# One table load, a sigmoid first, and other owners for the magnitudes of the weights

## The chip, the cores and the metric

The kernel runs on one core of a Trainium2 chip. The core has a matrix engine (TensorE, PE in the profile), VectorE (DVE), ScalarE (ACT), GpSimd (POOL) and SyncE (SP), which work side by side and wait for each other through semaphores. Times are device microseconds (us) of one execution; a kernel's time is the median of its runs. Lower is better.

## The reference

Sigmoid attention over 8 batches and 12 heads, sequence 448, head dimension 64, and an MLP on its output:

```python
scores = scale * np.matmul(q, k.transpose(0, 1, 3, 2)) - np.log(S)
attn = 1.0 / (1.0 + np.exp(-scores))
attn_out = np.matmul(attn, v)                       # -> x: (3584, 768)
h = x @ w_in                                        # 768 x 2048
g = np.where(h >= 1, h, np.where(h <= -1, 0.0, (h + 1) ** 2 / 4))
out = g @ w_out                                     # 2048 x 768
```

Inputs and output are float32.

## The kernel before

**The work.** A pair of heads fills the 128 partitions, so a batch is 6 pairs, 48 in all; each pair has four pieces of scores (three of 128 keys and one of 64). The MLP's inner dimension is cut into 16 chunks of 128. "Ups" multiply x by a chunk of w_in, "bend" applies the clipped quadratic, "downs" multiply by w_out. From the third batch on, the ups are done in blocks (L666). For the matmuls of ups and downs the operands are scaled and split into an fp16 high and low part.

**The weights.** The float32 weights arrive as words of 64 bits, two chunks' slots per transfer, in slots that borrow w_out's place in the on-chip memory (`w_out_sb`) or a `raww` tile. Chunk by chunk, `Weight.convert` does this for w_in (`wi`) and later for w_out (`wo`), with f the chunk:

- ScalarE's Prelu turns the high word into a float (L222);
- one step later VectorE shifts and merges the low word (L228, L229), and for some chunks takes the largest magnitude (L233, a reduce);
- one step after that, for the other chunks (`summed`), ScalarE takes the sum of magnitudes with an Abs and an accumulator (L215).

`find_scale` takes the scale of a group of eight chunks from these magnitudes, and `split` writes the fp16 parts: ScalarE the high one (L264), VectorE the low one (L265); for some chunks GpSimd takes part (L260 to L262). The transfers of w_in and the first four of w_out are issued by SP (L199), the later ones of w_out on ScalarE's own queue, from within `convert`. SP's slots must be free again: a slot of w_in's words is free when L229 has read it.

**The start.** Batch 0's attention uses float32 matmuls (L385 scores, L476 times v). ScalarE's sigmoid (L432) stands between the two, and its output of a pair is copied out (L482). In the same time w_in is converted. When batch 0's x is complete, `finish_x` splits it into `xhl`: ScalarE's L499, VectorE's L500. Then PE runs the ups (L700) and downs (L736) of batch 0, and w_out is converted beside them. From pair 8 on q, k and v are scaled and split as well; their magnitudes are ScalarE's L322 (into `hl` or `dump`), their split is L351.

**The second batch.** After batch 0's first downs come the ups of batch 1. Each chunk takes 18 matmuls L700 into one of three `ph` buffers; bend empties it: ScalarE L713, VectorE L714 and L715, then L716 and L717. In the same time VectorE computes the mixed weights for the later batches (L610 to L633), splits w_out (L265) and takes the maxima of x (L486).

**What sets the order.** A scheduler with a model of the machine sets the order of each engine's instructions, except where the code pins it: SP in the first part is in the order of the code, and what is passed to `tc.keep_in_program_order` keeps its place relative to the code's order.

Of the kernel before, what the change touches and what calls it, by code (L numbers as in the profile page):

```python
# [14 lines left out]
F32 = mybir.dt.float32  # L15
F16 = mybir.dt.float16
BF16 = mybir.dt.bfloat16
I32 = mybir.dt.int32
AF = mybir.ActivationFunctionType
# [4 lines left out]
P = 128  # L24
# [7 lines left out]
NFULL = 8  # L32
NHALF = 6

NA = 8
# [10 lines left out]
POOL_FROM = 6  # L46
WI_SUM = 2
WO_SUM = 0
MAX_ACT = 47
# [23 lines left out]
def sigmoid_attention_mlp(ctx: ExitStack, tc: tile.TileContext, first_qvk, qkv, w_in, w_out, out_t):  # L73
# [24 lines left out]

    nls = const.tile([P, 1], F32, name="nls")
    nc.vector.memset(nls, -math.log(S))  # L100


# [73 lines left out]
    class Weight:  # L176


        def __init__(self, dram, sb, name, spare):
            self.dram, self.sb, self.name, self.spare = dram.bitcast(I32), sb, name, spare  # L180
            self.words, self.at, self.loaded = {}, 0, 0
            self.scale, self.inv = [], []
            self.most = const.tile([P, 2, NFC], F32, name=name + "_most")
            nc.vector.memset(self.most, 0.0)
            mod = WI_SUM if name == "wi" else WO_SUM
            self.summed = [f for f in range(NFC) if mod and f % mod == 0 and f not in (NA - 1, NFC - 1)]

# [19 lines left out]
        def convert(self):  # L207

            f = self.at - 2
            if 0 <= f < NFC:  # L210
                w = self.words.pop(f)
                if f in self.summed:

                    dump = wo.f32(-1) if self is wi else w[:, :DM].bitcast(F32)
                    nc.scalar.activation(dump, self.f32(f), AF.Abs, accum_out=self.most[:, 1, f : f + 1])  # L215
                if self is wo:
                    self.load(3 if f == 3 else 1)
            f = self.at
            if f < NFC:

                high = self.words_of(f)[1].bitcast(F32)
                nc.scalar.activation(self.f32(f), high, AF.Prelu, scale=2.0**-112, alpha=-(2.0**32))  # L222
            f = self.at - 1
# [84 lines left out]
    def prep_a(p):  # L308
        if NFULL <= p < NPAIR and first_time("max", p):
# [3 lines left out]
            if p < MAX_ACT:  # L313
# [6 lines left out]
                for t in range(n):  # L320
                    rt = raws[p][:, t * S : 2 * S + VW if t == 2 else (t + 1) * S]
                    nc.scalar.activation(dump[:, : rt.shape[1]], rt, AF.Abs, accum_out=m[:, t : t + 1])  # L322
            for mt, rt in parts[: n - 1] if p >= MAX_ACT else ():
# [482 lines left out]
    with tc.manual_schedule(engines={mybir.EngineType.SP}):  # L806
# [6 lines left out]
        for i in range(LAG):  # L813
            scores([i])
        state["scored"] = LAG
        while at < NPIECE:
# [128 lines left out]
```

## Time and profile before

| | |
|---|---|
| median of 3 runs | 1183.58 us (1179.28 to 1185.38) |
| profiled execution | 1182.99 us, its span 1181.3 us |
| PE busy | 1146.3 us (97%) |
| VectorE busy | 824.9 us (70%) |
| ScalarE busy | 697.1 us (59%) |
| GpSimd busy | 321.6 us (27%) |
| mean granted clock of TensorE | 0.987 |

A line of the profile names the engine, the line of the kernel, the operation, the tile that is written and the tiles that are read; in brackets stands the idle time of the engine just before, and what ended it. "PEld" is the load of weights, which overlaps PE. "PEclk" is the granted clock as a share of full speed. A stretch's row gives each engine's busy time in it.

### The profile page before, as it was taken

Reading aid. Unit: us, or ns where it says so; the run is one execution under the profiler, and the core shown is the slowest. Engines: PE = TensorE matmul, PEld = TensorE weight load, DVE = VectorE, ACT = ScalarE, POOL = GpSimd, SP = SyncE. Lnnn points to the kernel's source line nnn. Section 1 sums busy time; section 2 is a strip of 40 time slices with the busy share of each in tenths; the row PEclk is TensorE's granted clock in tenths of the full one; section 3 lists DMA queues with packets and bytes.
Section 4 is the critical chain, followed back from the end, with each engine's and each line's share of the span. In section 5 each row is a group of like instructions: output and inputs, shape, how many; then the busy total and the mean of one; then the engine's idle time right before and its main releaser. Section 6 shows DMA issues by size and latency. Waiting matters only on the chain.

```text
span 1181.3 us, 20203 instructions
## 1 busy us (share of the span) xinstructions
PE 1146.3 (97%) x7662; PEld 669.0 (57%) x7662; DVE 824.9 (70%) x1760; ACT 697.1 (59%) x1158; POOL 321.6 (27%) x389
## 2 busy tenths in 40 slices
PE   5889999899999999999999999999999999999998
PEld 1224433344445776457755677457764677558954
DVE  4877999898945588467973689466883678736830
ACT  5975885665743587447763577546874486513410
POOL 0004310000332254325354236232534253310000
PEclk8899999899999999999999999999999999999999
DMA  9941544447532366224643165424552146302400
GB/s 361 335 150 61 195 149 132 151 142 244 176 109 64 119 213 212 64 64 150 253 146 100 33 251 193 132 64 141 196 207 68 61 155 223 117 25 98 153 16 32
DMA packets 58113, 170.01 MB, mean 144 GB/s; under 512 B 8608, under 2 KB 39840, under 8 KB 51872
## 3 DMA queue, kind: packets, MB, share of 16 engines
q1 hardware_dynamic: 56288, 159.29, 39.4%
q10 hardware_dynamic: 1728, 9.44, 2.3%
q8 instruction: 60, 0.98, 0.3%
q14 instruction: 37, 0.30, 0.1%
HBM read 126.94 MB, written 23.40 MB: 127 GB/s over the span
## 4 chain that ended last, share of the span: by engine, by line
PE 76%; DVE 9%; DMA 8%; ACT 4%; issue 1%; POOL 1%; SPq 0%; ACTq 0%; DVEq 0%
PE po L736 35%; PE ph L666 23%; PE pav L476 8%; PE psc L394 3%; PE psc L403 3%; DMA blocks<-mixs 2%; PE ph L700 2%; DMA w_out_sb<-w_in 2%; PE psc L389 1%; DMA raw<-qkv 1%; ACT a L432 1%; DVE g L714 1%; DMA w_out_sb<-w_out 1%; DMA w_in_sb<-blocks 1%; DVE mixs L624 1%
## 5 line engine op out<-in xcount | busy, mean ns | idle before, releaser
L736 PE MATMUL po<-ghl,w_out_sb 128*128 128x448 f16 x2304 | 445.7, 353 | 0.9 <-DVE g L715 0.9
L736 PEld LDWEIGHTS <-w_out_sb 128*128 128x128 f16 x2304 | 221.8, 98 | 216.6 <-issue 14.0
L666 PE MATMUL ph<-w_in_sb 128*128 128x224 f16 x3024 | 307.7, 259 | 2.0 <-DMA w_in_sb<-blocks 1.6
L666 PEld LDWEIGHTS <-w_in_sb 128*128 128x128 f16 x3024 | 282.6, 98 | 30.9 <-issue 27.4
L444 DVE SCALAR_TENSOR_TENSOR ahl<-psc,ahl 128x896 f16<-128x896 f32 (+1 forms) x170 | 152.9, 900 | 112.7 <-ACT ahl L443 110.4
L435 ACT ACTIVATE psc<-psc,nls,sqk 128x896 f32<-128x896 f32 (+1 forms) x136 | 129.4, 971 | 114.7 <-PE psc L403 97.2
L356 POOL TENSOR_SCALAR raw<-raw,qkv_s 128x448 f32<-128x448 f32 (+1 forms) x93 | 71.3, 781 | 452.9 <-DVE qkv_i L136 363.0
L443 ACT ACTIVATE ahl<-psc 128x896 f16<-128x896 f32 (+1 forms) x170 | 126.9, 762 | 32.9 <-DVE ahl L444 31.8
L700 PE MATMUL ph<-xhl,w_in_sb 128*128 128x448 f16 x576 | 115.5, 358 | 5.2 <-DVE xhl L500 2.9
L675 DVE TENSOR_TENSOR xhl<-ph,xhl 128x224 f32<-128x224 f32 x240 | 87.7, 382 | 26.2 <-PE ph L666 19.7
L322 ACT ACTIVATE dump<-raw 128x448 f16<-128x448 f32 (+1 forms) x105 | 61.8, 588 | 69.0 <-DMA raw<-qkv 68.0
L476 PE MATMUL pav<-ahl,v 128*64 128x448 f16 x748 | 95.6, 359 | 0.0
L713 ACT ACTIVATE g<-xhl,hr,ihr 128x448 f32<-128x448 f32 x96 | 68.7, 752 | 44.0 <-DVE xhl L675 43.1
L716 ACT ACTIVATE ghl<-g 128x448 f16<-128x448 f32 x128 | 72.7, 573 | 36.7 <-DVE g L715 36.3
L700 PEld LDWEIGHTS <-w_in_sb 128*128 128x128 f16 x576 | 55.9, 99 | 64.0 <-issue 16.4
L717 DVE TENSOR_TENSOR ghl<-g,ghl 128x448 f16<-128x448 f32 x128 | 85.6, 675 | 7.1 <-ACT ghl L716 6.6
L714 DVE SCALAR_TENSOR_TENSOR g<-g,rk 128x448 f32<-128x448 f32 x112 | 81.1, 739 | 10.7 <-ACT g L713 10.5
L746 DVE TENSOR_SCALAR o<-po,od 128x448 f32<-128x448 f32 x48 | 32.5, 679 | 65.8 <-PE po L736 65.6
L358 POOL TENSOR_TENSOR hl<-raw,hl 128x448 f16<-128x448 f32 x62 | 70.0, 1149 | 0.0
L394 PE MATMUL psc<-qk 128*128 128x448 f16 x252 | 66.6, 354 | 0.4 <-issue 0.3
L715 DVE SCALAR_TENSOR_TENSOR g<-xhl,ihs,g 128x448 f32<-128x448 f32 x96 | 65.5, 699 | 0.3
L385 PE MATMUL psc<-ghl 64*128 64x448 f32 (+1 forms) x128 | 37.4, 672 | 21.9 <-ACT a L432 17.1
(156 smaller groups left out, 1150.0 us busy)
## 6 DMA issues: line engine op xcount, KB each, us to landing
w_in_sb<-blocks SPq DMA_DIRECT2D x48, 1344.0 KB, 6.5
raw<-qkv SPq DMA_DIRECT2D x34, 704.0 KB, 4.9
qk<-hl SPq DMA_DIRECT2D x320, 56.0 KB, 2.0
w_out_sb<-w_in SPq DMA_DIRECT2D x16, 768.0 KB, 10.9
out_t<-o SPq DMA_DIRECT2D x48, 224.0 KB, 1.9
blocks<-mixs SPq DMA_DIRECT2D x8, 768.0 KB, 4.3
w_out_sb<-w_out ACTq DMA_DIRECT2D x6, 768.0 KB, 4.3
raww<-w_out ACTq DMA_DIRECT2D x6, 768.0 KB, 5.4
```

What stands on the lines that cost most here:

```text
L394: nc.tensor.matmul(out, kq[:, j, 1, w], kq[:, j, 0, :], start=True, stop=False)
L435: nc.scalar.activation(a, a, AF.Sigmoid, bias=nls, scale=sqk)
L443: nc.scalar.activation(hi, x, AF.Copy, scale=ATT)
L444: nc.vector.scalar_tensor_tensor(out=lo, in0=x, scalar=ATT, in1=hi, op0=ALU.mult, op1=ALU.subtract)
L476: nc.tensor.matmul(pav[j * D : (j + 1) * D, :S], *terms[j][t], start=c == 0 and t == 0, stop=mid and t == len(terms[j]) - 1,)
L666: nc.tensor.matmul(out, w[:, wt, wh, c * P : (c + 1) * P], xc[:, xt, c, xh, :], start=j in (0, 2) and c + wh + xh == 0, stop=c == HC - 1 a ...
L675: add = lambda out, q, other: nc.vector.tensor_tensor(out=out, in0=quarter(q), in1=other, op=ALU.add)
L700: nc.tensor.matmul(ph[:, :S], w_in_sb[:, f, wh, c * P : (c + 1) * P], xhl[:, c, xh, :], start=c == 0 and wh + xh == 0, stop=c == NCC - 1 a ...
L714: nc.vector.scalar_tensor_tensor(out=g, in0=g, scalar=rt, in1=g, op0=ALU.min, op1=ALU.mult)
L716: nc.scalar.activation(hi, g, AF.Copy)
L717: (nc.gpsimd if f % GPOOL else nc.vector).tensor_tensor(out=ghl[:, f, 1, :], in0=g, in1=hi, op=ALU.subtract)
L736: nc.tensor.matmul(po[:, :S], w_out_sb[:, f, wh, m * P : (m + 1) * P], ghl[:, f, gh, :], start=f == lo and wh + gh == 0, stop=f == hi - 1 ...
```

## The change

The constant tile `nls` gets a second column, and a sigmoid of one column stands ahead of all else on ScalarE. `scores([0])` is followed at once by the first conversion step, whose Prelu is pinned, so that the first real sigmoid stands ahead of it. The chunks whose magnitudes ScalarE takes are now listed: 8, 10, 12 of w_in (before 0, 2, 4, 6, 8, 10, 12, 14) and ten of w_out (before none). They are taken four steps after the Prelu and not two, are pinned in the order of the code, and write to a `tmp` tile for w_out. The raw maxima of the pairs 8 to 10 are pinned too.

```diff
-WI_SUM = 2
-WO_SUM = 0
+SUMS = (8, 10, 12), (0, 1, 2, 3, 4, 8, 9, 10, 11, 12)
+SUM_LAG = 4
...
-    nls = const.tile([P, 1], F32, name="nls")
+    nls = const.tile([P, 2], F32, name="nls")
     nc.vector.memset(nls, -math.log(S))
+    nc.scalar.activation(nls[:, 1:2], nls[:, 0:1], AF.Sigmoid)
+    nls = nls[:, 0:1]
...
-            mod = WI_SUM if name == "wi" else WO_SUM
-            self.summed = [f for f in range(NFC) if mod and f % mod == 0 and f not in (NA - 1, NFC - 1)]
+            self.summed = SUMS[name == "wo"]
...
         def convert(self):
+            f = self.at - SUM_LAG
+            if f in self.summed:
+                dump = wo.f32(-1) if self is wi else tmp_p.tile([P, S], F32, tag="tmp", name="dump").bitcast(F16)[:, :DM]
+                tc.keep_in_program_order(
+                    nc.scalar.activation(dump, self.f32(f), AF.Abs, accum_out=self.most[:, 1, f : f + 1])
+                )
             f = self.at - 2
             if 0 <= f < NFC:
-                w = self.words.pop(f)
-                if f in self.summed:
-                    dump = wo.f32(-1) if self is wi else w[:, :DM].bitcast(F32)
-                    nc.scalar.activation(dump, self.f32(f), AF.Abs, accum_out=self.most[:, 1, f : f + 1])
+                self.words.pop(f)
                 if self is wo:
                     self.load(3 if f == 3 else 1)
             f = self.at
             if f < NFC:
                 high = self.words_of(f)[1].bitcast(F32)
-                nc.scalar.activation(self.f32(f), high, AF.Prelu, scale=2.0**-112, alpha=-(2.0**32))
+                ins = nc.scalar.activation(self.f32(f), high, AF.Prelu, scale=2.0**-112, alpha=-(2.0**32))
+                if self is wi and f == 0:
+                    tc.keep_in_program_order(ins)
...
-                    nc.scalar.activation(dump[:, : rt.shape[1]], rt, AF.Abs, accum_out=m[:, t : t + 1])
+                    ins = nc.scalar.activation(dump[:, : rt.shape[1]], rt, AF.Abs, accum_out=m[:, t : t + 1])
+                    if p < NFULL + 3:
+                        tc.keep_in_program_order(ins)
...
         for i in range(LAG):
             scores([i])
+            if i == 0:
+                convert(wi, 1)
```

The lines of the changed kernel are shifted: L222 is L226 there, L322 is L328, L351 is L359, L432 is L440, L499 and L500 are L507 and L508, L610 is L618, L714 and L715 are L722 and L723.

The head of ScalarE's list, before (L222 the Prelu, L432 the sigmoid, L215 the Abs, `a` the sigmoid's output):

```order
L222 ACT_TABLE_LOAD
L222 ACTIVATE w_in_sb<-w_out_sb 128x768
L432 ACT_TABLE_LOAD
L432 ACTIVATE a_123<-psc,nls 128x896
L215 ACTIVATE w_out_sb,wi_most<-w_in_sb 128x768
L432 ACTIVATE a_128<-psc,nls 128x896
L222 ACTIVATE w_in_sb<-w_out_sb 128x768 x2
```

and of the change:

```order
L101 ACT_TABLE_LOAD
L101 ACTIVATE nls<-nls 128x1
L440 ACTIVATE a_124<-psc,nls 128x896
L226 ACTIVATE w_in_sb<-w_out_sb 128x768
L440 ACTIVATE a_130<-psc,nls 128x896
L226 ACTIVATE w_in_sb<-w_out_sb 128x768 x2
```

The second table load and the Abs are gone from this place, and the first sigmoid stands ahead of the first Prelu.

ScalarE's list before the splitting of batch 0's x (the rows after these are L499, in the change L507), before:

```order
L222 ACTIVATE w_out_sb<-w_out_sb 128x768
L264 ACTIVATE w_in_sb<-w_in_sb,wi_s 128x768
L432 ACTIVATE a_367<-psc,nls 128x896
L482 ACTIVATE x_91<-pav 128x448
L222 ACTIVATE w_out_sb<-w_out_sb 128x768
L432 ACTIVATE a_378<-psc,nls 128x896
L264 ACTIVATE w_in_sb<-w_in_sb,wi_s 128x768
L432 ACTIVATE a_416<-psc,nls 128x448
L432 ACTIVATE a_424<-psc,nls 128x896
L432 ACTIVATE a_442<-psc,nls 128x896
L482 ACTIVATE x_91<-pav 128x448
L432 ACTIVATE a_475<-psc,nls 128x896
```

and of the change:

```order
L328 ACTIVATE hl,m_371<-raw 128x448
L440 ACTIVATE a_378<-psc,nls 128x896
L440 ACTIVATE a_416<-psc,nls 128x448
L359 ACTIVATE hl<-raw,qkv_s 128x448 x2
L440 ACTIVATE a_424<-psc,nls 128x896
L328 ACTIVATE hl,m_428<-raw 128x448 x2
L215 ACTIVATE w_out_sb,wi_most<-w_in_sb 128x768
L440 ACTIVATE a_442<-psc,nls 128x896
L490 ACTIVATE x_92<-pav 128x448
L215 ACTIVATE w_out_sb,wi_most<-w_in_sb 128x768
L440 ACTIVATE a_475<-psc,nls 128x896
L215 ACTIVATE w_out_sb,wi_most<-w_in_sb 128x768
```

The raw maxima and splits of the pairs 8 and 9 and the three Abs of w_in now stand here; the Prelus of w_out's third and fourth chunk went behind the splitting of x.

VectorE's list at the second batch, around the first L715 (which empties the first `ph` buffer), before:

```order
L714 SCALAR_TENSOR_TENSOR g<-g,rk_1737 128x448 x2
L633 TENSOR_SCALAR mixp<-w_in_sb,mixes 128x2x384 x2
L633 TENSOR_SCALAR mixp<-w_in_sb,mixes 128x384 x2
L265 SCALAR_TENSOR_TENSOR w_out_sb<-w_out_sb,wo_s 128x768
L715 SCALAR_TENSOR_TENSOR g<-ph,ihs_1741,g 128x448 x2
L714 SCALAR_TENSOR_TENSOR g<-g,rk_1737 128x448
L610 TENSOR_TENSOR mixa<-w_in_sb 128x768 x2
```

and of the change, in which the four L633 (there L641) stand further ahead:

```order
L618 TENSOR_TENSOR mixa<-w_in_sb 128x768
L271 SCALAR_TENSOR_TENSOR w_out_sb<-w_out_sb,wo_s 128x768
L618 TENSOR_TENSOR mixa<-w_in_sb 128x768
L722 SCALAR_TENSOR_TENSOR g<-g,rk_1748 128x448 x3
L622 TENSOR_TENSOR mixa<-mixa 128x384
L494 TENSOR_REDUCE xm<-x_92 128x1
L723 SCALAR_TENSOR_TENSOR g<-ph,ihs_1752,g 128x448 x3
```

A third L714, the second pair of L610, the second L614 and the second L486 moved from behind the first L715 to ahead of it.

## The prediction

> **What bounds the kernel now.** I read the page first, then PE's waits, then the stretches, then the order of time where PE waits. The page's first line and the granted clock in its 40 slices:
>
> ```profile
> PE 1146.3 (97%) x7662; PEld 669.0 (57%) x7662; DVE 824.9 (70%) x1760; ACT 697.1 (59%) x1158; POOL 321.6 (27%) x389
> PEclk8899999899999999999999999999999999999999
> ```
>
> PE is busy for 1146.3 of 1181.3 us, so all but 35.0 us of the span is matmul time; the change leaves every matmul as it is. A gain can only come out of those 35.0 us and out of time at a reduced clock, and both lie in the first slices and in one later one (the 8 among the clock's nines, at some 206 to 236 us). PE's waits name the places (us in total, times, longest):
>
> ```profile
> PE psc L385 <- ACT a L432: 17.1, 8, 4.2
> PE ph L700 <- DVE xhl L500: 2.9, 1, 2.9
> PE ph L700 <- DVE g L715: 1.9, 1, 1.9
> ```
>
> Half of the idle time is batch 0's scores waiting for ScalarE's sigmoid. The stretches (us, then busy time of PE, PEld, DVE, ACT, POOL, the granted clock, DMA share, GB/s) show how full the other engines are:
>
> ```profile
> 10.00:20.00 10.00, 7.92 (x22) 1.88 (x24) 5.15 (x7) 7.58 (x11) 0.00 (x0) 0.66 1.02 413
> 40.00:50.00 10.00, 6.86 (x31) 2.10 (x33) 8.84 (x19) 10.00 (x18) 0.00 (x0) 0.96 1.04 401
> 50.00:60.00 10.00, 10.00 (x32) 2.33 (x30) 9.73 (x18) 10.00 (x16) 0.00 (x0) 0.70 0.66 205
> 72.00:76.40 4.40, 4.13 (x14) 0.99 (x14) 4.40 (x7) 3.81 (x6) 0.00 (x0) 0.62 0.01 4
> 140.00:160.00 20.00, 19.86 (x98) 8.00 (x97) 19.03 (x43) 16.04 (x26) 1.31 (x1) 1.00 0.45 134
> 216.00:223.00 7.00, 4.90 (x14) 2.02 (x14) 7.00 (x14) 4.35 (x6) 0.00 (x0) 0.53 0.14 39
> 220.00:240.00 20.00, 19.88 (x97) 8.75 (x96) 19.93 (x48) 10.77 (x15) 1.72 (x1) 0.92 0.17 70
> ```
>
> To 50 us the DMA is full; from 40 to 60 ScalarE has no idle time; VectorE is nearly full from 40 to 60 and again from 140 to 160 and 220 to 240. PE's idle time and its clock hang together: two pieces at 72 and at 216 us run at 0.62 and 0.53.
>
> **The start, part by part.** The head of the program in order of time (start us, us, engine, line, and in brackets the idle time before and its releaser):
>
> ```profile
> 0.80 1.28 ACT L222 ACT_TABLE_LOAD   x1 [0.80 <-PEq L937]
> 4.51 3.36 PE L385 MATMUL psc<-ghl 64*128 64x448 f32 x8 [4.51 <-DMA ghl<-first_qvk]
> 8.81 0.89 ACT L222 ACTIVATE w_in_sb<-w_out_sb 128x768 f32<-128x768 f32 x1 [6.73 <-DMA w_out_sb<-w_in]
> 9.72 1.28 ACT L432 ACT_TABLE_LOAD   x1
> 11.02 1.01 ACT L432 ACTIVATE a<-psc,nls 128x896 f32<-128x896 f32 x1
> 12.08 1.86 PE L385 MATMUL psc<-ghl 64*128 64x448 f32 x4 [4.20 <-ACT a L432]
> ```
>
> ScalarE loads a table for the Prelu in time that is idle anyway, then a second one before the first sigmoid. With the dummy sigmoid one load remains, at 0.80, and the first sigmoid no longer stands behind a Prelu that waits for a transfer until 8.81. Its four matmuls are half of the eight that begin at 4.51, so sigmoid 0 can run at about 4.51 + 1.7 = 6.2 and not at 11.02, and PE's 4.20 us wait goes. On the removed load the row says 1.28 us, and the sigmoid starts 1.30 us after it. The Trainium skill (ScalarE: Activation LUTs, What ACT_TABLE_LOAD costs) puts a switch at 2.66 us, drain included; this trace shows no such drain behind the load, and by the page the sum below would be at most 1.4 us lower.
>
> This head start isn't worth 4.8 us at the end, because the next rows of ScalarE are the Prelus, one per chunk of w_in, and these wait for chunks that land at the pace of a full DMA. The last group of three before chunk 15 and its transfer time (median us to landing):
>
> ```profile
> 36.67 4.10 SPq L199 DMA_DIRECT2D w_out_sb<-w_in  x3
> w_out_sb<-w_in SPq DMA_DIRECT2D x4, 768.0 KB, 10.8
> 49.59 0.91 ACT L222 ACTIVATE w_in_sb<-w_out_sb 128x768 f32<-128x768 f32 x1
> 69.61 0.89 ACT L222 ACTIVATE w_out_sb<-w_out_sb 128x768 f32<-128x768 f32 x1 [2.67 <-DMA w_out_sb<-w_out]
> 73.00 0.92 ACT L222 ACTIVATE w_out_sb<-w_out_sb 128x768 f32<-128x768 f32 x1 [0.35 <-DMA w_out_sb<-w_out]
> 72.27 0.98 PE L385 MATMUL psc<-ghl 64*64 64x448 f32 x4 [3.59 <-ACT a L432]
> ```
>
> Chunk 12 is issued at 36.67 and is there at about 36.67 + 10.8 = 47.5; its Prelu runs at 49.59. ScalarE, freed of five magnitude passes and of the raw maxima, can be waiting for it, so this point moves by **-2.1 us**, not by more. From there to the splitting of x (L499) ScalarE's list changes. Durations from start to start, from a piece in which it never idles:
>
> ```profile
> 53.32 1.25 ACT L351 ACTIVATE hl<-raw,qkv_s 128x448 f16<-128x448 f32 x2
> 54.43 0.65 ACT L432 ACTIVATE a<-psc,nls 128x448 f32<-128x448 f32 x1
> 54.95 0.93 ACT L222 ACTIVATE w_in_sb<-w_out_sb 128x768 f32<-128x768 f32 x1
> 55.74 0.86 ACT L215 ACTIVATE w_out_sb<-w_in_sb 128x768 f32<-128x768 f32 x1
> 56.57 0.95 ACT L264 ACTIVATE w_in_sb<-w_in_sb,wi_s 128x768 f16<-128x768 f32 x1
> L322 ACT ACTIVATE dump<-raw 128x448 f16<-128x448 f32 (+1 forms) x105 | 61.8, 588 | 69.0 <-DMA raw<-qkv 68.0
> ```
>
> Two L351 take 54.43 - 53.32 = 1.11, a Prelu 0.79, an Abs with its accumulator 0.83, an L322 0.59, and a split I take as long as the Abs. Counted in the two orders, the stretch gains four L322 (2.36), two L351 (1.11) and one Abs (0.83), and loses two w_out Prelus (1.58, now behind L499) and one split (0.83): **+1.9**. Against it stand the waits for w_out, 2.67 + 0.35 = 3.0 now. SP issues the first two w_out chunks right behind the last of w_in, and ScalarE reaches their Prelus some 12 us behind chunk 12; with the same slots to be freed by VectorE's L229 I leave 1.7 of the 3.0 standing, so **-1.3** (bounds: 0 and -3.0). Last, PE's 3.59 us wait is followed by the stretch at 0.62: 4.40 x 0.38 = 1.7 us lost at the end of batch 0, and with ScalarE no longer stuck there I take **-1.6**. The start then is -2.1 + 1.9 - 1.3 - 1.6 = **-3.1 us**. Bounds: -9 (the raw maxima fit into waits, +1.9 becomes -2, and 3.0 and 1.7 go whole), and +2 (VectorE gets four more reduces in w_in's first group, 4 x 0.86 = 3.4 us in stretches where it is 5.2 to 8.8 of 10 busy; that is hidden while ScalarE is the later one, and if it isn't, find_scale and every split behind it come later by that much, and the gain at chunk 12 with them).
>
> **The magnitudes of w_out.** Ten passes go from VectorE to ScalarE:
>
> ```profile
> L215 ACT ACTIVATE w_out_sb<-w_in_sb x8: 832/845/866, 11.9 to 61.2; 128x768 f32<-128x768 f32 x8
> L233 DVE TENSOR_REDUCE wo_most<-w_out_sb x16: 940/946/953, 64.9 to 184.3; 128x1 f32<-128x768 f32 x16
> ```
>
> About even in price: VectorE -8.6 us, ScalarE +8.3 us between 90 and 190 us. There PE waits for nobody (it is busy 19.86 of 20), and ScalarE has 4 us of room in each 20. I cost this edit at **0**; what hides it is PE's own queue of L700 and L736. If the cover is gone, it is the third rival.
>
> **The handover to batch 1's ups.** The order is made anew, and it moves VectorE's work where PE already waits:
>
> ```profile
> 214.42 0.74 PE L700 MATMUL ph<-xhl,w_in_sb 128*128 128x448 f16 x3
> 218.10 6.11 PE L700 MATMUL ph<-xhl,w_in_sb 128*128 128x448 f16 x18 [2.93 <-DVE xhl L500]
> 235.38 2.81 PE L700 MATMUL ph<-xhl,w_in_sb 128*128 128x448 f16 x14
> 214.63 0.96 DVE L610 TENSOR_TENSOR mixa<-w_in_sb 128x768 f32<-128x768 f16 x1 [1.72 <-DMA blocks<-mixs]
> 234.05 1.27 DVE L715 SCALAR_TENSOR_TENSOR g<-ph,ihs,g 128x448 f32<-128x448 f32 x2
> 235.83 1.82 DVE L610 TENSOR_TENSOR mixa<-w_in_sb 128x768 f32<-128x768 f16 x2
> 238.17 0.61 DVE L486 TENSOR_REDUCE xm<-x 128x1 f32<-128x448 f32 x1
> 239.82 0.55 DVE L614 TENSOR_TENSOR mixa<-mixa 128x384 f32<-128x384 f32 x1
> ```
>
> The three ph buffers are filled by 54 L700; the 55th (at 235.38) needs the first L715, the first of two, done at 234.05 + 0.64 = 234.7. That leaves 0.7 us of slack. In the new order a third L714, a second pair of L610, a second L614 and a second L486 stand ahead of the first L715 instead of behind it: 0.6 (as an L715, of the same shape) + 1.8 + 0.5 + 0.5 = 3.4 us. VectorE is full there (19.93 of 20), so the first L715 comes 3.4 later and the 55th L700 2.7 later, whatever PE does before it: four score matmuls moved ahead of L700 only shift where it waits. A PE idle of 2.93 and one of 3.59 us were each followed by a stretch at about half clock; at 216 us it cost 7.00 x 0.47 = 3.3. I add one such stretch: 2.7 + 3.3 = **+6.0 us**. Bounds: -6.2 (VectorE, lighter by 8.6 us, doesn't wait 1.72 for blocks and splits x early: the 2.93 and the 3.3 both go) and +8 (another wait of the 1.9 us kind on L715). I take the value near the upper end because the row that decides, the full VectorE, is the one that the new order lengthens. On the clock the Trainium skill (TensorE: Matmul & The Clock Gate, What's actually happening) says that the array drops to half after an idle window of about 3.4 us, free-running. Two drops here came after 3.59 and 2.93 us, so the trace agrees only roughly; by the page alone a 2.7 us wait could pass without a drop, and the sum would be 3.3 lower.
>
> **The sum.** -3.1 + 0 + 6.0 = +2.9 on the profiled execution's 1182.99 us (span 1181.3 and 1.7 around it), which stands 0.6 below the median of 1183.58: **1185.9 us**, no change that the measurement can tell (0.5%, some 5.9 us, is what it can).
>
> **The rivals.**
> 1. *The handover improves* (faster). The 1.72 us wait for blocks shows that VectorE there waits for its own earlier work, and it loses 8.6 us of that; then the 2.93 and its half-clock stretch go, and the start keeps -3.1: 1182.99 - 3.1 - 6.2 = 1173.7. Against it: the 3.4 us moved ahead of L715.
> 2. *The head start is lost, the handover doesn't change* (same). ScalarE waits at w_in's landings, which don't move, and the raw maxima fill what it gained; VectorE's gain of 1.72 and PE's shorter first wait pay for the 2.7: 1183.
> 3. *The ten Abs hold up w_out's loads* (slower). They are pinned, and on ScalarE's queue each stands ahead of the next w_out load issued there; a late load means a Prelu that waits with sigmoids queued behind it. The row to price it is the wait that w_out's Prelu has now, 2.67, and an Abs of 0.83; if PE runs dry once, it is 3.5 and a half-clock stretch of 3.3 on top of the forecast: 1185.9 + 6.8 = 1192.7. It decides once ScalarE lags PE by more than the units that PE has queued; for it speaks ScalarE's 16 of 20 at 140 us, against it that PE has no wait at all there now.
>
> **How the numbers follow.** The forecast has 0.47, rival 1 0.20, rival 2 0.16, rival 3 0.17. The forecast's own range is 1181 to 1190.5 (the half-clock stretch that may not come, the start's bounds); a tenth in all lies over 1189.5. Faster by over 0.5% (under 1177.7) is rival 1: 0.20. Slower (over 1189.5) is rival 3 and the forecast's upper end, 0.17 + 0.10 = 0.27. The rest, 0.37 + 0.16, is 0.53. The range takes rival 1's middle and rival 3's: 1173.5 to 1194; some 0.1 lies on each side.
>
> **What would show it.** Right: one ACT_TABLE_LOAD; the first sigmoid near 6 us; the first L499 (there L507) about 3 us earlier than 84.79; ten Abs on w_out and no PE wait on ScalarE between 100 and 200 us; at the second batch a PE wait on L715's successor of 2.5 to 7 us and a stretch with the clock near 0.5 behind it. Wrong: the first L700 of the second batch without a wait and no reduced clock after 200 us (rival 1), a first L499 at 84 us or later (rival 2), or PE waits on Prelus or sigmoids at 100 to 200 us (rival 3).

## The result

The changed kernel takes **1191.34 us** (median; 1190.71 to 1193.12) against 1183.58 before: a ratio of 1.0071, with a 95% interval of 1.0051 to 1.0092. It is slower by 7.8 us, by more than the 0.5% that a measurement here can tell from no change. The profiled execution took 1190.71 us (span 1189.0) against 1182.99 (1181.3), so the two traces differ by 7.7 us, and these are followed here. The lines of the changed kernel are numbered 2 to 8 higher than before: L499/L500 are L507/L508, L714/L715 are L722/L723, L700 is L708, L610 is L618, L444 is L452.

The page's first line of the changed kernel:

```profile
PE 1143.3 (96%) x7662; PEld 668.4 (56%) x7662; DVE 820.9 (69%) x1755; ACT 699.8 (59%) x1168; POOL 319.6 (27%) x389
```

PE's busy time fell by 3.0 us and its idle time grew by 10.7, from 35.0 to 1189.0 - 1143.3 = 45.7 us. Four landmarks in PE's order of time tell where (start us, duration us, line, and how many instructions). Each row is the first of its kind at that place. First the kernel before:

```profile
87.50 2.82 PE L700 MATMUL ph<-xhl,w_in_sb 128*128 128x448 f16 x14
210.02 0.22 PE L172 MATMUL pm<-diag,one 128*128 128x128 bf16 x1
254.17 3.20 PE L736 MATMUL po<-ghl,w_out_sb 128*128 128x448 f16 x16
325.66 0.54 PE L736 MATMUL po<-ghl,w_out_sb 128*128 128x448 f16 x2
```

and the same places of the changed kernel:

```profile
81.60 2.63 PE L708 MATMUL ph<-xhl,w_in_sb 128*128 128x448 f16 x13
206.28 0.22 PE L174 MATMUL pm<-diag,one 128*128 128x128 bf16 x1
256.02 1.30 PE L744 MATMUL po<-ghl,w_out_sb 128*128 128x448 f16 x6
333.10 3.19 PE L744 MATMUL po<-ghl,w_out_sb 128*128 128x448 f16 x16
```

| place | after minus before, us | what this part added |
|---|---|---|
| first ups of batch 0 | -5.9 | the start: -5.9 |
| maximum of batch 1's x | -3.7 | w_out's stretch: +2.2 |
| first downs of batch 1, behind its first eight chunks' ups | +1.9 | the handover to batch 1: +5.6 |
| downs behind its second eight chunks' ups | +7.4 | the stretch behind it: +5.5 |
| end | +7.7 | the other 850 us: +0.3 |

The figures of the last column are differences of the rounded ones beside them. In w_out's stretch PE waits 1.8 us where it waited 0.3 before. At the handover it waits 9.8 us where it waited 3.1. In the stretch behind it, it waits 4.9 us where it waited 3.2, and the greater part of that loss is time at a lowered clock. Nearly all of the waiting is for VectorE; two short waits at the handover, 0.60 and 0.55, are for ScalarE. The main ones in PE's order of time, with the idle time and its releaser in brackets:

```profile
107.61 2.43 PE L708 MATMUL ph<-xhl,w_in_sb 128*128 128x448 f16 x12 [1.55 <-DVE g L723]
216.40 11.11 PE L708 MATMUL ph<-xhl,w_in_sb 128*128 128x448 f16 x51 [3.72 <-DVE xhl L508]
235.98 0.17 PE L158 MATMUL pm<-mb,one 128*128 128x3 bf16 x1 [4.55 <-DVE g L723]
322.25 1.28 PE L397 MATMUL psc<-hl,w_in_sb 128*128 128x448 f16 x3 [3.32 <-DVE ahl L452]
```

VectorE of the same kernel in order of time, ahead of the first, the second and the fourth of these waits:

```profile
103.34 1.31 DVE L722 SCALAR_TENSOR_TENSOR g<-g,ru 128x448 f32<-128x448 f32 x1
104.58 2.39 DVE L235 SCALAR_TENSOR_TENSOR w_out_sb<-w_out_sb 128x768 int32<-128x768 int32 x1
106.89 0.67 DVE L723 SCALAR_TENSOR_TENSOR g<-ph,ihs,g 128x448 f32<-128x448 f32 x1
...
212.93 1.83 DVE L618 TENSOR_TENSOR mixa<-w_in_sb 128x768 f32<-128x768 f16 x2 [3.18 <-DMA blocks<-mixs]
214.74 1.01 DVE L271 SCALAR_TENSOR_TENSOR w_out_sb<-w_out_sb,wo_s 128x768 f16<-128x768 f32 x1
215.67 0.68 DVE L508 SCALAR_TENSOR_TENSOR xhl<-x,x_s,xhl 128x448 f16<-128x448 f32 x1
...
316.61 1.38 DVE L625 SCALAR_TENSOR_TENSOR mixa<-mixa,mixes 128x384 f32<-128x384 f32 x1
317.92 1.79 DVE L632 SCALAR_TENSOR_TENSOR mixs<-mixa,mixes,mixs 128x768 f16<-128x768 f32 x1
319.63 1.57 DVE L722 SCALAR_TENSOR_TENSOR g<-g,rk 128x448 f32<-128x448 f32 x1
321.12 1.08 DVE L452 SCALAR_TENSOR_TENSOR ahl<-psc,ahl 128x896 f16<-128x896 f32 x1
```

At 212.93 VectorE stands for 3.18 us (1.72 before) at an addition of the mixed weights, because its buffer is still being read by a transfer; the split of x that PE needs, L508, is queued behind it. At 316.61 three passes of mixing and bend, 4.5 us together, stand ahead of the one low part (L452) that PE waits for. And the stretches of the clock (columns as in the prediction; the granted clock is the third number from the end):

```profile
216.40:227.40 11.00, 11.00 (x51) 5.24 (x50) 11.00 (x25) 5.17 (x7) 2.53 (x1) 0.88 0.10 29
236.50:243.00 6.50, 6.43 (x27) 2.98 (x27) 5.92 (x16) 3.68 (x7) 0.00 (x0) 0.77 0.01 3
321.00:324.36 3.36, 2.11 (x9) 0.59 (x8) 3.36 (x6) 0.61 (x2) 0.63 (x2) 0.57 0.78 242
324.36:333.10 8.74, 8.74 (x38) 4.08 (x37) 8.54 (x17) 5.10 (x8) 0.00 (x0) 0.77 0.93 310
```

After each of the three longer waits PE runs at a lowered clock. Time lost to it is PE's busy time times (1 - clock): 1.3 and 1.5 at the handover, and 1.1 + 2.0 around 322 to 333 (in the third row PE is still waiting for the first 1.25 us; from 322.25 on its clock is 0.50). The 36 ups there take 8.74 us where before had 6.81 at full clock (318.85 to 325.66).

### The profile page after: what moved, and what is told of

The parts are those of the page before. It is cut to its first block, busy times and chain, and to the rows that moved or that the text cites. A ratio compares the mean times of both kernels' runs of the same rounds, so it can differ in the third digit from the quotient of the medians.

```text
span 1189.0 us, 20209 instructions
## 1 busy us (share of the span) xinstructions
PE 1143.3 (96%) x7662; PEld 668.4 (56%) x7662; DVE 820.9 (69%) x1755; ACT 699.8 (59%) x1168; POOL 319.6 (27%) x389
## 4 chain that ended last, share of the span: by engine, by line
PE 75%; DVE 9%; DMA 8%; ACT 5%; issue 1%; POOL 1%; SPq 1%; ACTq 0%; POOLq 0%; DVEq 0%
PE po L744 33%; PE ph L674 24%; PE pav L484 8%; PE psc L402 3%; DMA w_out_sb<-w_in 3%; PE psc L411 3%; PE ph L708 2%; PE psc L397 2%; DMA w_out_sb<-w_out 1%; DMA raw<-qkv 1%; DMA blocks<-mixs 1%; ACT a L440 1%; DVE g L722 1%; DVE mixa L618 1%; DVE g L723 1%
## 5 line engine op out<-in xcount | busy, mean ns | idle before, releaser
L452 DVE SCALAR_TENSOR_TENSOR ahl<-psc,ahl 128x896 f16<-128x896 f32 (+1 forms) x170 | 152.7, 899 | 112.9 <-ACT ahl L451 110.8
L708 PE MATMUL ph<-xhl,w_in_sb 128*128 128x448 f16 x576 | 118.4, 363 | 6.2 <-DVE xhl L508 3.7
L328 ACT ACTIVATE dump<-raw 128x448 f16<-128x448 f32 (+1 forms) x105 | 61.8, 589 | 79.1 <-DMA raw<-qkv 78.1
L683 DVE TENSOR_TENSOR xhl<-ph,xhl 128x224 f32<-128x224 f32 x240 | 87.5, 382 | 26.2 <-PE ph L674 19.7
L708 PEld LDWEIGHTS <-w_in_sb 128*128 128x128 f16 x576 | 56.0, 100 | 73.6 <-issue 27.7
L725 DVE TENSOR_TENSOR ghl<-g,ghl 128x448 f16<-128x448 f32 x128 | 86.4, 682 | 7.5 <-ACT ghl L724 7.0
L722 DVE SCALAR_TENSOR_TENSOR g<-g,rk 128x448 f32<-128x448 f32 x112 | 80.0, 730 | 10.4 <-ACT g L721 10.1
L723 DVE SCALAR_TENSOR_TENSOR g<-xhl,ihs,g 128x448 f32<-128x448 f32 x96 | 66.2, 707 | 0.3
L484 PEld LDWEIGHTS <-v 128*64 128x64 f16 x748 | 36.3, 109 | 38.2 <-issue 23.5
```

The costliest lines, as they stand in the source:

```text
L452: nc.vector.scalar_tensor_tensor(out=lo, in0=x, scalar=ATT, in1=hi, op0=ALU.mult, op1=ALU.subtract)
L484: nc.tensor.matmul(pav[j * D : (j + 1) * D, :S], *terms[j][t], start=c == 0 and t == 0, stop=mid and t == len(terms[j]) - 1,)
L683: add = lambda out, q, other: nc.vector.tensor_tensor(out=out, in0=quarter(q), in1=other, op=ALU.add)
L708: nc.tensor.matmul(ph[:, :S], w_in_sb[:, f, wh, c * P : (c + 1) * P], xhl[:, c, xh, :], start=c == 0 and wh + xh == 0, stop=c == NCC - 1 a ...
L722: nc.vector.scalar_tensor_tensor(out=g, in0=g, scalar=rt, in1=g, op0=ALU.min, op1=ALU.mult)
L723: nc.vector.scalar_tensor_tensor(out=g, in0=h, scalar=ihs, in1=g, op0=ALU.mult, op1=ALU.max)
```

## The experiments

Two accounts were open: that the loss is VectorE's queue at batch 1, whose order the scheduler made anew, or that it lies in what the edits themselves cost (ScalarE's ten passes, the loads behind them, the start). Each expectation gives them in numbers. In the kernels with more lines the same instructions stand a few lines further down (L723 of the change is L725 or L726, L452 is L453). The runs came in three sets; each set has its own runs of the kernel before beside it.

### 1. The sigmoid first, and nothing else

The kernel before with the dummy sigmoid, the pinned Prelu and its earlier call:

```diff
+    nc.scalar.activation(nls[:, 1:2], nls[:, 0:1], AF.Sigmoid)
+    nls = nls[:, 0:1]
...
+                if self is wi and f == 0:
+                    tc.keep_in_program_order(ins)
...
+            if i == 0:
+                convert(wi, 1)
```

> The kernel before with three edits of the change alone: the dummy sigmoid (one table load), the first conversion step right behind the first scores, and the pinned first Prelu. Magnitudes stay as before. Theory A (the start's 6 us came from ScalarE's lighter list: raw maxima and Abs moved into late waits): first ups matmul within 1.5 us of 87.5, time 1182 to 1184. Rival (the 6 us came from the early first sigmoid): first ups matmul near 81.6, time near 1177.6.

Measured: 1182.57 us, ratio 0.9998 (0.9982 to 1.0015). The first ups of batch 0 stand at 87.73, before at 87.50. One table load less and a first sigmoid 4.7 us earlier (6.30 against 11.02) are worth nothing by themselves: they are gone before the first ups.

### 2. Only w_out's magnitudes to ScalarE

The kernel before with the ten pinned Abs on w_out, four chunks behind (its w_in as before):

```diff
+            if name == "wo":
+                self.summed = [0, 1, 2, 3, 4, 8, 9, 10, 11, 12]
...
+            f = self.at - 4
+            if self is wo and f in self.summed:
+                dump = tmp_p.tile([P, S], F32, tag="tmp", name="dump").bitcast(F16)[:, :DM]
+                tc.keep_in_program_order(
+                    nc.scalar.activation(dump, self.f32(f), AF.Abs, accum_out=self.most[:, 1, f : f + 1])
+                )
```

> The kernel before with the ten w_out magnitudes on ScalarE alone, four steps late; two table loads and w_in as before. Theory A (the loss is VectorE's order at the second batch, which this move re-makes): start as before, at the second batch a PE wait of 4 to 5 us for the first ph buffer and a half-clock stretch, about +6.4: 1190, or 1194 if the wait near 320 us comes too. Rival B (the ten Abs themselves hold ScalarE and w_out's loads up): PE waits between 100 and 200 us, and they make up the loss. Rival C (the loss belongs to w_in's part): 1183.6, no change.

Measured: 1190.92 us, ratio 1.0071 (1.0054 to 1.0088): the whole loss of the change, without its start. PE at the handover of this kernel, in order of time:

```profile
220.60 12.31 PE L708 MATMUL ph<-xhl,w_in_sb 128*128 128x448 f16 x51 [4.30 <-DVE xhl L508]
240.18 0.17 PE L156 MATMUL pm<-mb,one 128*128 128x3 bf16 x1 [3.35 <-DVE g L723]
```

VectorE's order there is that of the changed kernel, instruction for instruction, with 3.77 us of waiting for `blocks` ahead of the split of x. Between 100 and 200 us PE never waits for ScalarE. From the first ups to the first downs of batch 0 it takes 79.8 us, with no wait of PE; the kernel before takes 79.1. So the ten Abs hold nothing up in w_out's stretch, and rival 3 of the prediction falls. The order that comes with them goes with 8 us more; its two short waits for ScalarE at the handover, 0.60 and 0.55, are in it.

### 3. The change, but w_out's magnitudes left to VectorE

```diff
-SUMS = (8, 10, 12), (0, 1, 2, 3, 4, 8, 9, 10, 11, 12)
+SUMS = (8, 10, 12), ()
```

> The change with w_out's magnitudes left on VectorE (none on ScalarE); all else as changed. Theory A: start as in the change (first ups matmul near 81.6, -6.0 against before); at the second batch one pair L610 less ahead of the first L715 than in the change, so the loss there is 2 to 4 us in place of 6.4: 1180 to 1183. Rival B (the Abs on ScalarE are the loss): all of it gone, 1177 to 1178.

Measured: 1189.29 us, ratio 1.0051 (1.0036 to 1.0065). The first ups are at 81.59, so the start's gain of 5.9 us is there and is lost again: PE waits 2.77 us for L508 and 2.60 and 2.17 us for L723 at the handover, and 3.21 us for L452 near 320. The order's account, in the form that w_out's move alone brings it, fell with this run: the same waits come without w_out's move. It isn't one edit that spoils the handover. Each of the two halves makes the scheduler put the mixing somewhere else, and both put it in PE's way.

### 4. The change with batch 1's split kept ahead of the mixing

Of the change nothing is taken back. The scales of batch 1's x come with priority, and the splits of x, the first additions of the mixing and bend's L723 of batch 1 keep the order of the code:

```diff
+X1_PRIO = 593
...
+            if b == 1:
+                tc.keep_in_program_order(ins)
...
-            (nc.gpsimd if r < MIXP else nc.vector).tensor_tensor(
+            tc.keep_in_program_order((nc.gpsimd if r < MIXP else nc.vector).tensor_tensor(
...
-    inv_x = finish_x(1)
-    common_scales(1, inv_x)
+    with tc.high_priority(offset=X1_PRIO):
+        inv_x = finish_x(1)
+        common_scales(1, inv_x)
```

> The change with all its parts, and beside it: the splitting of batch 1's x and its scales get the scheduler's high priority, and the x splits, the first additions of the weight mixing and the bends' maxima of batch 1 are pinned in program order on VectorE. Same arithmetic. Theory A: the waits of 3.7 and 4.6 us at the second batch fall under 2 us in all and the half-clock stretches there go, -10 to -12 against the change: 1179 to 1181, or 1174 to 1176 if the wait near 322 us goes too. Rival B (the ten Abs): stays at 1189 or above.

Measured: 1178.77 us, ratio 0.9957 (0.9942 to 0.9973), 12.6 us below the median of the change. VectorE and PE at the handover, then PE near 310, in order of time:

```profile
208.60 0.68 DVE L509 SCALAR_TENSOR_TENSOR xhl<-x,x_s,xhl 128x448 f16<-128x448 f32 x1
...
209.50 4.15 PE L711 MATMUL ph<-xhl,w_in_sb 128*128 128x448 f16 x21
...
225.54 1.87 PE L485 MATMUL pav<-a,v 128*64 128x448 f32 x8 [1.03 <-ACT a L441]
...
310.40 1.28 PE L398 MATMUL psc<-hl,w_in_sb 128*128 128x448 f16 x3 [3.39 <-DVE ahl L453]
```

The first ups of batch 1 start without a wait and at full clock. PE is 9.0 us ahead of before's trace at the first downs of batch 1 (245.19 against 254.17), and only 4.4 at the downs behind its second eight chunks (321.30 against 325.66). Between them lies the wait that stands at 322 in the changed kernel: its 3.39 us are followed by a stretch at 0.53. This shows that the order in VectorE's queue makes the handover's loss. The wait near 310 is a second cause, which was not yet explained.

### 5. The kernel before with the same pins

The pins of experiment 4, with before's own lines:

```diff
+X1_PRIO = 593
...
+            if b == 1:
+                tc.keep_in_program_order(ins)
...
+            tc.keep_in_program_order((nc.gpsimd if r < MIXP else nc.vector).tensor_tensor(
...
+    with tc.high_priority(offset=X1_PRIO):
+        inv_x = finish_x(1)
+        common_scales(1, inv_x)
```

> The kernel before with the same pins and priority for batch 1's x as in the run before, nothing of the change. Theory A (the second batch's wait is a matter of VectorE's order, whoever takes the magnitudes): the wait of 2.93 us and its half-clock stretch go, so 5 to 9 us are gained at the second batch, less what a wait near 315 us takes back: 1177 to 1181, about the time of the change with pins plus what is left of its start. Rival (the pins only repair what the change broke): 1183, as before.

Measured: 1180.62 us, ratio 0.9981 (0.9968 to 0.9994). The waits at the handover (2.93 and 1.88 in the kernel before) go here too, and a wait of 2.04 us for GpSimd's split of v comes at 312. So the pins are a gain of their own, of which the change has no share: 2 to 3 us of the 4.4 in experiment 4.

### 6. The wait near 310: a pair taken from GpSimd

Experiment 4 with one more pair split by ScalarE and VectorE, not by GpSimd, so that GpSimd doesn't work beside VectorE there:

```diff
-QA = 17
+QA = 18
```

> The pinned change, with pair 17's split of q, k and v on ScalarE and VectorE and no longer on GpSimd (one constant, 17 to 18). Same arithmetic. In the pinned change PE waits 3.4 us near 310 us for VectorE while GpSimd runs these splits, and VectorE's additions take 1.4 to 1.5 us in place of 0.6. Theory A (GpSimd's passes slow VectorE's, and that makes the wait): VectorE's passes there take their usual time, the wait falls below 2 us and the half-clock stretch goes, -3 to -5: 1174 to 1176. Rival (VectorE simply has too much to do there): three more passes on it, the wait grows, 1179 to 1181.

Measured: 1179.34 us, ratio 0.9978 (0.9961 to 0.9995). VectorE's passes ahead of the wait run at 0.55 to 0.62 us where experiment 4 has 1.44 and 1.50:

```profile
305.36 1.44 DVE L730 TENSOR_TENSOR ghl<-g,ghl 128x448 f16<-128x448 f32 x1
306.73 1.50 DVE L625 TENSOR_TENSOR mixa<-mixa 128x384 f32<-128x384 f32 x1
```

(both rows from experiment 4, in order of time). So the slow passes come from GpSimd working beside them. Still PE waits 0.90 and 1.94 us for the same low parts, and the clock goes to 0.72 again. VectorE still stands 1.55 us (1.87 in experiment 4) at an addition of the mixing that waits for `blocks`, and it now makes three splits of pair 17 as well. The overlap is a part of that wait and not the whole of it; the time did not improve.

### 7 and 8. The other halves of the start, one execution each

In the kernel before, first only the raw maxima pinned, then only w_in's magnitudes as in the change (chunks 8, 10 and 12 on ScalarE, four steps behind their Prelu):

```diff
+                    if p < NFULL + 3:
+                        tc.keep_in_program_order(ins)
```

```diff
-WI_SUM = 2
-WO_SUM = 0
+SUMS = (8, 10, 12), ()
+SUM_LAG = 4
```

> The kernel before with the raw maxima of pairs 8 to 10 pinned and nothing else of the change. Only the start is read: the first ups matmul, 87.5 us before and 81.6 with the change. Theory A1 (the raw maxima filled the waits at the end of batch 0): 82 to 84. Theory A2 (the fewer Abs of w_in did it): 87 to 88.

> The kernel before with w_in's magnitudes as in the change (8, 10, 12 on ScalarE, four steps late, the first group on VectorE) and nothing else of it. Only the start is read: the first ups matmul. Theory A1 (the raw maxima did it): 86.5 to 88. Theory A2 (the fewer Abs did it): 82 to 84.

Measured, one execution each: 1188.36 and 1185.58 us. The first ups are at 82.17 and 84.25, so each of them gains at the start what the sigmoid alone does not, and both lose it at batch 1: PE waits 3.3 and 3.9 us there for the split of x, then 1.84 and 2.17 us for L717 in experiment 7 and 1.18 us for L716 in experiment 8, which are bend's L715. Experiment 7 comes out as its theory A1 says and experiment 8 near its A2 (84.25 where 82 to 84 was expected), so neither edit is the only source of the start's gain. Single executions say nothing on a per cent, but the waits are in the rows.

### 9. The later mixings moved

Experiment 4 with the last three mixings issued at steps 72, 78 and 86 of batch 1, not 56, 65 and 75:

```diff
-MIX0 = 8
-MIX1 = 85
+MIXU = (8, 17, 27, 36, 46, 72, 78, 86)
...
-                    while mixed_at < NFC // 2 and u >= MIX0 + mixed_at * (MIX1 - MIX0) // (NFC // 2):
+                    while mixed_at < NFC // 2 and u >= MIXU[mixed_at]:
```

> The change with the pins and the priority for batch 1's x, and the last three of the eight mixings of weights begun behind the second group's ups (steps 72, 78, 86 in place of 56, 66, 76). Same arithmetic. Theory A (each late wait is VectorE's queue headed by a mixing): the wait near 310 us falls under 1.5 us without a half-clock stretch, and 4 to 5 us are gained on the pinned change: 1173 to 1175. Rival (VectorE is short of time there whatever its order): the wait moves to another place, 1177 to 1180.

Measured: 1176.77 us, ratio 0.9957 (0.9941 to 0.9973), between the two expectations. The wait at 310 is gone: with the mixing out of its way, L452 is in time. Two waits of 2.0 us for the magnitudes of pairs (qkv_e) stand near 299 and 350 instead. What is left of w_out's stretch shows in this kernel's order of time (GpSimd, VectorE, PE), with the window behind it:

```profile
105.67 2.00 POOL L268 TENSOR_TENSOR w_in_sb<-w_in_sb 128x768 f16<-128x768 f32 x1
...
106.10 2.38 DVE L235 SCALAR_TENSOR_TENSOR w_out_sb<-w_out_sb 128x768 int32<-128x768 int32 x1
108.41 0.67 DVE L725 SCALAR_TENSOR_TENSOR g<-ph,ihs,g 128x448 f32<-128x448 f32 x1
...
109.13 3.81 PE L710 MATMUL ph<-xhl,w_in_sb 128*128 128x448 f16 x12 [2.74 <-DVE g L725]
```

```profile
109.00:114.00 5.00, 4.87 (x18) 1.86 (x17) 4.29 (x8) 3.85 (x6) 1.82 (x2) 0.66 0.00 0
```

The merge of w_out's low word (L235, 0.95 us on average for the chunks of w_in) takes 2.38 us while GpSimd subtracts, bend's L725 stands behind it, and PE loses 2.74 us and 1.7 us of clock. The change has the same at 107.61, with 1.55 and no drop of the clock. From the first ups to the first downs of batch 0 this kernel takes 84.3 us, the kernel before 79.1.

### 10. The kernel before with the pins and the mixings moved

The diffs of experiments 5 and 9, both in the kernel before:

```diff
+X1_PRIO = 593
+MIXU = (8, 17, 27, 36, 46, 72, 78, 86)
...
+                    while mixed_at < NFC // 2 and u >= MIXU[mixed_at]:
```

> The kernel before with the same pins, priority and later mixings, nothing of the change. Theory A: both waits gone there as well, 1176 to 1179, and the difference to the changed kernel with the same pins is what the change is worth by itself, the 3 to 6 us of its start. Rival (the change is worth nothing by itself): the same time as the changed kernel with pins, within 1.5 us.

Measured: 1177.77 us, ratio 0.9963 (0.9950 to 0.9976). With the same pins and mixings in both, the change is worth 1176.77 against 1177.77, which these runs cannot tell apart: the rival's forecast. The trace has a surprise at the start. ScalarE's order up to the first ups is that of the kernel before, yet they stand at 84.53, not at 87.50. The window of 70 to 80 us, of the kernel before:

```profile
70.00:80.00 10.00, 7.73 (x28) 2.00 (x28) 7.73 (x10) 7.48 (x10) 0.00 (x0) 0.83 0.19 76
```

and of this one:

```profile
70.00:80.00 10.00, 9.10 (x42) 2.65 (x44) 7.92 (x12) 8.35 (x11) 0.00 (x0) 1.00 0.08 30
```

The stretch at a lowered clock isn't always there. Experiments 1, 2 and 5 have it, with first ups at 87.5 to 87.7; this one has not. All kernels that have the change's whole start are at 81.6 to 82.3 in their traces. So the start gains 6 us against an execution with that stretch and about 3 us against this one. Only about half of the 3 us between the two is the clock. The other 1.4 us come earlier: ScalarE waits 1.57 and 0.25 us for w_out's transfers (2.67 and 0.35 before), and PE then 2.50 us for the sigmoid, not 3.59. Experiments 1, 2 and 5, which have the stretch, have waits of 3.27 to 3.74 there.

### 11. Experiment 9 with w_out's magnitudes left to VectorE

```diff
-SUMS = (8, 10, 12), (0, 1, 2, 3, 4, 8, 9, 10, 11, 12)
+SUMS = (8, 10, 12), ()
```

> The changed kernel with pins and later mixings, but w_out's magnitudes all on VectorE as before. Theory A (w_out's move is worth nothing where its cover holds, as the prediction costed it): within 1.5 us of the kernel with the ten Abs on ScalarE. Rival (VectorE's 8.6 us are needed at the second batch): a wait of 1 to 3 us on VectorE returns there, 3 to 6 us slower.

Measured: **1174.19 us**, ratio 0.9934 (0.9919 to 0.9950), the fastest of all, 6.7 us below the median before in its set (1180.93). PE's wait in w_out's stretch and three windows of it:

```profile
111.39 2.43 PE L710 MATMUL ph<-xhl,w_in_sb 128*128 128x448 f16 x12 [1.05 <-DVE g L725]
```

```profile
111.00:116.00 5.00, 4.61 (x24) 1.96 (x24) 3.50 (x5) 3.48 (x6) 3.29 (x2) 1.00 0.00 0
205.00:235.00 30.00, 30.00 (x153) 12.79 (x151) 27.80 (x67) 21.18 (x32) 3.09 (x3) 1.00 0.25 84
300.00:330.00 30.00, 30.00 (x171) 14.82 (x170) 28.15 (x40) 19.44 (x32) 18.15 (x20) 1.00 0.26 69
```

PE is full at the handover and near 310, at full clock. Against experiment 9 only w_out's magnitudes differ, and the median is 2.6 us lower without their move, which neither expectation had. The two intervals overlap, so the size is uncertain. In the traces the wait of 2.74 us goes, but two others, 1.18 and 1.05, come at 125 and 133. At the first downs of batch 1 the two traces are 2.1 us apart (246.88 and 244.77); the rest arises behind them, where experiment 9 alone has its two waits of 2.0.

Against experiment 10 the start's edits differ, and the median is 3.6 us lower. The traces don't have this at the start: experiment 11 is 2.6 us ahead at the first ups (81.89 against 84.53), level at the first downs of batch 1 (244.77 against 244.65), and 3.2 ahead at the downs behind its second eight chunks (314.28 against 317.43), because experiment 10 waits 2.19 us for a pair's magnitudes at 297 and runs at a lowered clock behind that. That the 3.6 us are the start's own gain is not shown.

## Why the prediction was right and wrong

The forecast of 1185.9 us was 5.4 us low. The time lies in the range of 1173.5 to 1194, but beyond the forecast's own 1181 to 1190.5 and beyond the bound for no change, on the side that had 0.27. Two terms of the sum came near, one of them partly by luck; the largest part of the miss is a place that had no term. Step by step:

- **What bounds the kernel: right.** Nearly all of the difference is PE's idle time and the clock behind it, at the start, beside w_out and at batch 1.
- **The start, forecast -3.1: the right sign, too small.** Measured -5.9. The Prelu of chunk 12 moved by -1.7 (49.59 to 47.92; forecast -2.1), and w_out's two waits shrank from 3.02 to 1.92, -1.1 (forecast -1.3). The step that failed in size is the tail: before, four waits of ScalarE behind 77 us (1.33, 0.84, 0.47 and 2.01, for scores and scales) add to 4.65 us; after, 0.61 is left. The added Abs and raw maxima, priced at +1.9 on ScalarE's path, ran in these waits, so the tail gave -4.0 where -1.6 was put down: -1.7 + 1.9 - 1.1 - 4.0 = -4.9, and ScalarE's split of x begins 5.2 us earlier. ScalarE of the kernel before, first and last of these waits, in order of time:

```profile
77.49 1.01 ACT L432 ACTIVATE a<-psc,nls 128x896 f32<-128x896 f32 x1 [1.33 <-PE psc L385]
...
84.79 2.35 ACT L499 ACTIVATE xhl<-x,x_s 128x448 f16<-128x448 f32 x4 [2.01 <-DVE x_s L132]
```

and of the changed one, its only wait in that stretch, and the split of x:

```profile
70.03 1.23 ACT L359 ACTIVATE hl<-raw,qkv_s 128x448 f16<-128x448 f32 x2 [0.61 <-DVE qkv_i L138]
...
79.62 3.46 ACT L507 ACTIVATE xhl<-x,x_s 128x448 f16<-128x448 f32 x6
```

Experiment 10 adds that some 3 us of the 5.9 are not there against every execution of the old order: the transfers of w_out came sooner there, and the lowered stretch stayed away. Of the removed table load, experiment 1 shows that nothing is left at the first ups: as argued, the Prelus behind it wait for w_in's landings (the second instruction of its ScalarE that waits is the first Prelu, 1.51 us, until 8.81 as before).
- **w_out's magnitudes, 0: right as far as experiment 2 shows; the +2.2 belongs to the start.** From the first ups to the first downs of batch 0 (400 matmuls in each kernel) it takes 79.1 us before and 79.8 with w_out's move alone (experiment 2), but 82.1 in the change and, without the move, 81.1 and 82.8 (experiments 3 and 11). So the head start was wrongly counted in full up to the end: of its 5.9 us 2.9 are lost by the first downs of batch 0, 2.2 by the maximum of batch 1's x, and no term stood for that. The wait of the change in it, 1.55 us, is for VectorE: a merge falls beside a pass of GpSimd, with bend behind it. That the loss comes from the Prelus of w_out that now stand behind the splitting of x is likely, but no run separates it. In the pinned kernels the move itself may cost up to 2.1 us more (9 against 11).
- **The handover, +6.0: right in place and cause, near in size partly by luck.** Measured +5.6, made up otherwise. Forecast were 2.7 us of waiting and 3.3 for one more lowered stretch. Measured are 6.7 more of waiting (9.8 against 3.1) and no more lowered time than before: 2.8 us lost against 2.6. (The prediction's 3.3 counts in time in which PE was still waiting.) PE's wait for L723 was 4.55, not 2.7. The wait for the split of x grew to 3.72, where it was taken as unchanged: PE comes there 2.5 us earlier, the split only 1.7. The mechanism (mixing ahead of the first L715) is as forecast: from the start of the first split of x to that of the first L723 (L715) it was 234.05 - 217.37 = 16.7 us before and 235.26 - 215.67 = 19.6 after, +2.9, where 3.4 was counted. The two rows of VectorE that the prediction does not show, first of the kernel before, then of the change:

```profile
217.37 0.68 DVE L500 SCALAR_TENSOR_TENSOR xhl<-x,x_s,xhl 128x448 f16<-128x448 f32 x1
...
235.26 1.85 DVE L723 SCALAR_TENSOR_TENSOR g<-ph,ihs,g 128x448 f32<-128x448 f32 x3
```

- **The missing term, +5.5.** The sum ended at 254 us. The order was made anew behind that, too, and at 317 to 321 two mixing passes and a bend went ahead of L452; beside GpSimd's passes they took 4.5 us, where some 2.2 are usual. The kernel before already waited 0.42 and 1.88 us near there, at full clock throughout. The change waits 1.8 us more in this stretch and loses some 3.0 to the clock. The prediction's bound of "another wait of the 1.9 us kind" had no place for it, and it is the miss: -2.8 at the start, +2.2 at w_out, -0.4 at the handover, +5.5 here and +0.3 behind make 4.8 us, and 1185.9 + 4.8 = 1190.7, the profiled execution.
- **Rival 1** (the handover improves) needed the order to stay: with the pins it comes (1178.8, and 1174 to 1177 with the mixings moved). **Rival 2** (the head start is lost) didn't happen as told, but has a part in it: 3.7 of the 5.9 us reach the maximum of batch 1's x at 206 us. **Rival 3** named nearly the right size, 1192.7, for a mechanism that isn't there: between 90 and 200 us PE waits 0.2 us for ScalarE and never for a load.

## What to carry to other kernels

Where a scheduler sets the order, an edit at one place has to be read at every later place where PE comes within a few microseconds of waiting: list what stands in the in-order queue ahead of the instruction PE needs, and look first for one that waits for a transfer. Price such a wait with the stretch of lowered clock behind it, and look also past the first bad place. Pin the order at those places before judging an edit elsewhere: the same edits to the start went with 6 us more unpinned (experiment 3), and with 3.6 us less when both kernels were pinned (11 against 10). Even then follow the head start from place to place: there it was gone by 245 us, and the gain arose behind.

## What the runs showed of the hardware

**VectorE beside GpSimd.** A pass of VectorE with two operands in SBUF (the on-chip memory of the tiles) can take 1.8 to 3.1 times as long beside a subtraction of GpSimd: L722 1.57 us where it is 0.67 alone, L632 1.79 against 1.00, L235 2.39 against 0.95, and in the kernel before one L714 2.06 against 0.67 (at 109 us, beside L262). GpSimd's rows of the change, beside VectorE's above:

```profile
104.15 2.00 POOL L268 TENSOR_TENSOR w_in_sb<-w_in_sb 128x768 f16<-128x768 f32 x1
...
316.19 2.70 POOL L366 TENSOR_TENSOR hl<-raw,hl 128x448 f16<-128x448 f32 x2
318.85 1.86 POOL L366 TENSOR_TENSOR v<-raw,v 128x512 f16<-128x512 f32 x1
```

L444, which has one of its operands in PSUM (where TensorE writes), takes 1.07 us beside such a subtraction (L358, at 314 us of the kernel before) and 1.08 without it. The Trainium skill (SBUF — State Buffer, SBUF: two separate sides) says that VectorE instructions with two SBUF inputs and GpSimd ones that read SBUF exclude each other through a shared pair of ports, the later one waiting for the whole of the other. The rows agree in kind: it is the passes with two operands there that lengthen, by 0.8 to 1.4 us, no more than one GpSimd pass.

**The clock.** It was lowered behind waits of 2.74 (0.66), and of 0.90 and 1.94 within 4 us (0.72), and not behind single waits of 1.55 and 1.05 (1.00). One of 2.55 in experiment 6, at the place where experiment 9 has its 2.74, was not followed by a lowered clock, and one of 2.19 in experiment 10 was; so the length of a wait alone doesn't decide. Cut at the right places, the rows of every trace here show the clock at 1.00 or 0.50 and nothing between, in pieces of 3.41 us or a whole multiple of it (the ends of a trace aside); a figure between is a mean over pieces. Two neighbouring pieces of experiment 9, then of experiment 6 (the first number behind the comma is PE's busy time):

```profile
106.60:110.00 3.40, 0.87 (x5) 0.48 (x5) 3.40 (x4) 0.89 (x2) 1.07 (x1) 1.00 0.00 0
110.02:113.42 3.40, 3.40 (x12) 1.17 (x9) 2.72 (x5) 2.62 (x5) 1.64 (x1) 0.50 0.00 0
...
106.91:110.32 3.41, 1.63 (x9) 0.87 (x9) 3.41 (x5) 1.65 (x3) 0.32 (x1) 1.00 0.00 0
110.33:113.74 3.41, 3.41 (x20) 1.58 (x18) 2.69 (x5) 2.19 (x4) 2.01 (x2) 1.00 0.00 0
```

What counts is how much of one such piece PE stands idle: 2.5 us there, 1.8 here. From the first ups on, the 13 traces have 15 pieces at full clock with 2.0 us or more of idle time, and a piece at half clock follows on each of them. Of some 4000 with less than 1.79 us it follows on one (213.04 to 216.45 of the kernel before, 1.29 us idle), and of the five between on three. So a wait that is shared between two pieces can be free of this, while the same wait within one costs up to 1.7 us more, half of 3.41, or 3.4 where two pieces follow. The Trainium skill (TensorE: Matmul & The Clock Gate, What's actually happening) gives an idle window of about 3.4 us that runs freely; the pieces agree with it in length, but in this kernel a window that was idle for some 2 of its 3.4 us was enough.
